# Attention ahead of two feed-forward layers: weight tiles two passes later, six biases on another engine, three units' scores in other banks

## The chip, the core and the metric

The kernel runs on one core of a Trainium2 chip. A core has five engines that each work through a queue of their own in order: TensorE (PE; matrix products and transposes into PSUM banks, with its weight loads shown as PEld), VectorE (DVE), ScalarE (ACT), GpSimd (POOL) and SyncE (SP), which here only issues transfers. They wait for each other by semaphores. The metric is the device time of one execution in microseconds.

## The reference

Three things in a row, with 4 x 576 = 2304 tokens, 8 heads of 64, model width 512 and hidden width 2048:

```python
scores = scale * q @ k.T                       # per batch and head
scores = where((rel >= 0) & (rel < 128), scores + slopes * -abs(rel), -1e9)
attn = exp(scores - max);  attn = attn / (sum(attn) + 1e-9);  x = attn @ v
h = x @ w_in;   g = where(h > 0, h, exp(min(h, 0)) - 1);  x = g @ w_out    # layer 0
h = x @ w2_in;  g = h / (1 + exp(-h));                    out = g @ w2_out # layer 1
```

The inputs are float64; the kernel receives them as pairs of 32-bit words and must turn each weight into floats itself. It works with split numbers: a value is a high half (rounded) plus a low half (value minus high), and a product is three matmuls (high x high, high x low, low x high).

## The kernel before, in words

**Attention (lines 329 to 706).** Two neighbouring groups of 128 tokens (t) and a pair of heads (hp) are one unit; there are 36, numbered u, four head pairs to a t. The main loop (line 644) makes one turn, here called a pass, for each u from 0 to 38, and works on several units at once. In pass u:

- TensorE computes the scores of unit u (line 501; from unit 16 on line 504, with split numbers), for even u the value products of units u-4 and u-3 (line 585), and the transposes of unit u-2 (line 542).
- VectorE adds the bias to the scores and takes the maximum (line 518, "reduction"), inverts the sums of unit u-1 (lines 526 and 527) and copies half of the transposes of unit u-2 (line 553).
- ScalarE takes the exponentials of unit u (line 523), copies the value products (line 591) and the other half of the transposes (line 555).
- GpSimd normalizes unit u-1 (line 566) and, later on, copies keys (line 110).

The score banks are `s0` and `s1`, one each (line 496), so a unit's scores wait until the reduction of the unit before has read its bank. The bias of head h (line 437) is made from `rel`: heads 0 and 1 ahead of the loop, the others three each in passes 0 and 1 (line 696), all on VectorE.

**Weight tiles.** `weight_step` (line 190) works through a list of tasks, one per tile of 512 x 128 weights: load (line 118, SyncE), `rescale` (GpSimd and ScalarE), `sign` and `join` (VectorE, lines 149 and 154), `part` (ScalarE makes the high half, line 162; VectorE the difference, line 167, which is the low half, run from `owed`). It is called twice in each pass that is in the list `WSLOTS`; `u + 1` in the call is how many tasks may be loaded by then. In passes 0 to 14 the ten tiles of the first sweep come (five of `w_in`, then five of `w_out`), in passes 26 to 33 three more.

**Fill.** When the attention of a block of tokens is done, its feed-forward work is put into the list `fill`: five hidden tiles (`h`, line 244, four pieces each), then four output groups (`y`, line 302, five pieces each). Block 0 has 256 tokens, the others 512. Each pass puts in some pieces at three points (`PIECES`), strictly in order of the list; a piece is held back while its weights are not in `known` (line 693), and then all behind it wait too. A hidden tile is followed by four steps: ScalarE's exponential (line 251), VectorE's two steps (257, 258), ScalarE's high half (266) and VectorE's low half `gl` (272), which the y pieces read. The splits of a block's input into high and low (`split_x`, lines 227 and 228) stand at the end of the passes in which its value products come: 4 and 6 for block 0, 12 and 14 for block 1, 20 and 22 for block 2, 28 and 30 for block 3, two splits (a pair) in each.

**After attention (line 708).** The rest of `fill`, and then all further steps, run back to back on TensorE.

Of the kernel before, what the change touches and what calls it, by code (L numbers as in the profile page):

```python
# [8 lines left out]
F32 = mybir.dt.float32  # L9
# [5 lines left out]
ALU = mybir.AluOpType  # L15
PSUM = bass.MemoryType.PSUM

P = 128
# [24 lines left out]
def attention_elu_silu_kernel(  # L43
# [14 lines left out]
    nc = tc.nc  # L58
    NT, DM = out.shape
    B, H, S, D = shape  # L60
# [5 lines left out]
    scale = 1.0 / float(D) ** 0.5  # L66
# [17 lines left out]
    LAG = 2  # L84
    NR = 4
    PLAIN = 16
    WSLOTS = [*range(15), *range(26, 34)]
    PIECES = (2, 1, 2)
    BANKS = 3
    UNITS = [(t, hp) for t in range(NG // 2) for hp in range(NPAIR)]  # L90
# [12 lines left out]
    ps_ms = [ctx.enter_context(tc.tile_pool(name="ps_m", bufs=BANKS, space=PSUM))]  # L103
# [86 lines left out]
    def weight_step(loaded=0, which=(4, 2, 3, 1), lag=1, last=64, apart=(1, 0, 1)):  # L190


        for i in which:
            if (stage[i] < min(last, stage[i - 1]) and (i < len(stages) or fits(stage[i]))
                    and calls[0] >= at[i - 1][stage[i]] + (lag, *apart)[i - 1]):
                if i == len(stages):
                    made[tasks[stage[i]][0]] += 1
                stages[i - 1](*tasks[stage[i]])
                at[i][stage[i]] = calls[0]
                stage[i] += 1  # L200
        while stage[0] < (loaded or min(stage[-1] + NRAW, len(tasks))):
            load_w(*tasks[stage[0]])
            at[0][stage[0]] = calls[0]
            stage[0] += 1
# [124 lines left out]
    def attention():  # L329

        with ExitStack() as actx:
# [6 lines left out]
            ps_s = actx.enter_context(tc.tile_pool(name="ps_s", bufs=1, space=PSUM))  # L338
# [85 lines left out]
            rel = store[1][0][:, 0, 0:2 * P]  # L424
# [7 lines left out]
                clear(i, nc.gpsimd)  # L432
            bias = const.tile([P, H, 2 * P], BF16, tag="bias", name="bias")

            def make_bias(h):

                nc.vector.tensor_scalar(bias[:, h, :], rel, -(2.0 ** (-8.0 * (h + 1) / H)) / scale, None, op0=ALU.mult)

            make_bias(0)
            make_bias(1)  # L440
            cuts = {}

            def make_cuts():
# [44 lines left out]
            def scores(u):  # L488
                t, hp = UNITS[u]
                z, zq = kk[hp], qs.pop(u, None)  # L490
                pt = ps_[u] = p_p.tile([P, 2, 2, 2 * P], F32, tag="p", name="p")
                neg = st_p.tile([P, 4], F32, tag="neg", name="neg")
                sm = sums[u] = st_p.tile([P, 2, 2], F32, tag="sm", name="sm")
                es = []
                for j in range(2):
                    ps = ps_s.tile([P, 2, 2 * P], F32, tag=f"s{j}", name=f"s{j}")
                    for e in range(2):
                        c0 = first_col(2 * t + e)
                        cut = 2 * t + e in MID
                        if u < PLAIN:  # L500
                            nc.tensor.matmul(ps[:, e, c0:2 * P], qz[:, u % 4, j, e * P:(e + 1) * P],  # L501
                                             kz[:, u % 4, e * P + c0:(e + 2) * P], start=True, stop=not cut)
                        for x in range(0 if u < PLAIN else 2):
                            nc.tensor.matmul(ps[:, e, c0:2 * P], zq[:, j, e * P:(e + 1) * P],  # L504
                                             z[:, x, j, e * P + c0:(e + 2) * P], start=(x == 0), stop=(x == 1 and not cut))
                        if cut:
                            nc.tensor.matmul(ps[:, e, c0:2 * P], ident16, cuts[MID[2 * t + e]][:, c0:2 * P],
                                             start=False, stop=True)
                    for e in range(2):
                        g = 2 * t + e  # L510
                        i = 2 * j + e
                        c0 = AFTER.get(g, first_col(g))
                        src = ps[:, e, c0:2 * P]
                        dst = pt[:, j, e, c0:2 * P]
                        if g in AFTER:

                            nc.vector.memset(pt[:, j, e, 0:c0], 0.0)
                        nc.vector.tensor_tensor_reduce(  # L518
                            dst, src, bias[:, 2 * hp + j, c0:2 * P], -scale, 3.0e38, ALU.add, ALU.min,
                            neg[:, i:i + 1])  # L520
                        es.append((dst, neg[:, i:i + 1], sm[:, e, j:j + 1]))
                for dst, m, a in es:
                    nc.scalar.activation(dst, dst, AF.Exp, bias=m, scale=-1.0, accum_out=a)  # L523
# [120 lines left out]
            for u in range(NU + 3):  # L644
                known.update(weights)
                calls[0] += 1
                last = 2 * FIRST_F + (u >= 20) * NRAW
                if u in WSLOTS:
                    weight_step(min(u + 1, last), (4, 1), 2, last)
                pop()  # L650
                if u < NU:
                    scores(u)
# [3 lines left out]
                while owed:  # L656
                    owed.pop(0)()
                if u in WSLOTS:
                    weight_step(min(u + 1, last), (2, 3), 1, last)
                pop()  # L660
                evict = keep = None
                if u % 2 == 0 and u >= 4:
# [30 lines left out]
                                made_ready += [group(hidden(bi, f), 1, n, lambda i, f=f: (0, 0, f) in known)] * NKC  # L693
                            made_ready += outputs_of(bi)
                split_q(u + 2)
                if u < 2:
                    for h in range(2 + 3 * u, 5 + 3 * u):
                        make_bias(h)
                if u == 3:
                    make_cuts()  # L700
                point(PIECES[2])
# [114 lines left out]
```

## Time and profile before

| | |
|---|---|
| median of three runs | 923.42 us (923.14 to 923.63) |
| the profiled execution | 923.78 us, its span 922.1 us |
| busy in the span: PE, DVE, ACT, POOL | 909.7, 572.3, 434.0, 228.7 us |
| chain that ended last | PE 88%, DVE 4%, issue 3%, POOL 2%, ACT 2%, DMA 1% |
| largest lines of that chain | y L302 40%, h L244 39% |

A row of a timeline gives start and length of an instruction (or of several of the same kind that follow each other, with xN), its engine, line, operation and tiles (out<-in); in brackets stands how long the engine was idle before it and which instruction ended that wait. On TensorE each float32 product of scores, transposes and values is recorded as two. Instructions that overlap in the pipeline have lengths that add up to more than the time they take; the difference of two starts is the safer measure.

### The profile page before, as it was taken

To read this page: it belongs to the slowest core of one execution; us is meant where nothing else is said; L and a number is where in the kernel's file an instruction comes from. 1 tells how busy PE (TensorE), PEld (TensorE's weight loads), DVE (VectorE), ACT (ScalarE), POOL (GpSimd) and SP (SyncE) were. 2 spreads that over 40 slices of the span, in tenths; PEclk is the share of its full clock that TensorE was granted. 3 is DMA by queue.
4 is the path that set the end of the run, shared out by engine and by line. 5 is a ranking of instruction groups with operands and counts; after the bars stand their busy time and mean duration, and the time that the engine had idled before them with its cause. 6 is when DMAs were issued, how large, how long until landed. Compare 5 with 4: busy or idle time off the path is not lost.

```text
span 922.1 us, 12993 instructions
## 1 busy us (share of the span) xinstructions
PE 909.7 (99%) x4754; PEld 760.6 (82%) x4754; DVE 572.3 (62%) x1186; ACT 434.0 (47%) x959; POOL 228.7 (25%) x316
## 2 busy tenths in 40 slices
PE   7999999999999999999999999999999999999998
PEld 5878888887878888889888888888888888888887
DVE  7996888893777776576555556644366554444422
ACT  7776677764555434333343255543533342233311
POOL 5543555553444202220012022220221021000000
PEclk9999999999999999999999999999999999999999
DMA  9534335320242202210002012210221010000011
GB/s 271 184 100 114 103 99 173 99 64 10 90 130 91 69 1 70 69 46 1 1 17 76 23 46 71 71 43 23 69 69 47 1 46 0 35 35 23 23 46 46
DMA packets 45247, 59.81 MB, mean 65 GB/s; under 512 B 3328, under 2 KB 38912, under 8 KB 45184
## 3 DMA queue, kind: packets, MB, share of 16 engines
q1 hardware_dynamic: 45024, 58.86, 20.7%
q8 instruction: 37, 0.61, 0.3%
q14 instruction: 26, 0.21, 0.1%
q10 hardware_dynamic: 160, 0.13, 0.1%
HBM read 54.26 MB, written 4.72 MB: 64 GB/s over the span
## 4 chain that ended last, share of the span: by engine, by line
PE 88%; DVE 4%; issue 3%; POOL 2%; ACT 2%; DMA 1%; SPq 0%; POOLq 0%; DVEq 0%; ACTq 0%
PE y L302 40%; PE h L244 39%; PE a L585 3%; PE pt L542 3%; PE s L501 2%; PE s L504 2%; POOL wl L164 1%; POOL wraw L142 1%; DVE p L518 1%; DMA y<-in_k_dram 1%; DVE gl L272 0%; DMA wraw<-in_moe_w_in_dram 0%; ACT p L523 0%; DVE wraw L154 0%; DVE e L257 0%
## 5 line engine op out<-in xcount | busy, mean ns | idle before, releaser
L244 PE MATMUL h<-xh,wh 128*128 128x512 f32 (+1 forms) x640 | 238.6, 373 | 0.0
L244 PE MATMUL h<-xl,wh 128*128 128x512 f32 (+1 forms) x640 | 235.9, 369 | 0.6 <-DVE xl L228 0.6
L244 PE MATMUL h<-xh,wl 128*128 128x512 f32 (+1 forms) x640 | 235.8, 368 | 0.0
L164 POOL TENSOR_TENSOR wl<-wraw,wh 128x512 fp32r<-128x512 f32 x54 | 75.6, 1402 | 401.3 <-ACT wh L162 401.3
L272 DVE TENSOR_TENSOR gl<-e,gh 128x512 fp32r<-128x512 f32 (+1 forms) x158 | 106.0, 671 | 105.0 <-ACT gh L266 104.7
L251 ACT ACTIVATE e<-h 128x512 f32<-128x512 f32 (+1 forms) x160 | 87.9, 550 | 174.5 <-PE h L244 153.5
L266 ACT ACTIVATE gh<-e 128x512 fp32r<-128x512 f32 (+1 forms) x160 | 94.0, 587 | 107.6 <-DVE e L258 65.0
L244 PEld LDWEIGHTS h<-xh,wh 128*128 128x128 f32 x640 | 120.8, 189 | 20.4 <-issue 1.2
L244 PEld LDWEIGHTS h<-xl,wh 128*128 128x128 f32 x640 | 120.8, 189 | 20.0 <-DVE xl L228 0.8
L244 PEld LDWEIGHTS h<-xh,wl 128*128 128x128 f32 x640 | 120.6, 188 | 20.1
L302 PE MATMUL y<-gh,wh 128*128 128x512 f32 (+1 forms) x320 | 121.3, 379 | 0.2 <-ACT y L310 0.2
L302 PE MATMUL y<-gl,wh 128*128 128x512 f32 (+1 forms) x320 | 118.4, 370 | 1.0 <-DVE gl L272 1.0
L302 PE MATMUL y<-gh,wl 128*128 128x512 f32 (+1 forms) x320 | 118.0, 369 | 0.0
L302 PE MATMUL y<-wh,gh 128*128 128x512 f32 (+1 forms) x294 | 113.3, 385 | 0.0
L302 PE MATMUL y<-wl,gh 128*128 128x512 f32 (+1 forms) x294 | 113.2, 385 | 0.0
L302 PE MATMUL y<-wh,gl 128*128 128x512 f32 (+1 forms) x294 | 113.2, 385 | 0.0
L566 POOL TENSOR_SCALAR p<-p,sm 128x256 f32<-128x256 f32 (+2 forms) x144 | 71.0, 510 | 98.8 <-DVE sm L527 61.2
L260 DVE TENSOR_TENSOR e<-h,e 128x512 f32<-128x512 f32 (+1 forms) x80 | 50.9, 637 | 60.4 <-ACT e L251 59.8
L162 ACT ACTIVATE wh<-wraw 128x512 fp32r<-128x512 f32 x58 | 38.5, 667 | 91.0 <-DVE wraw L154 66.7
L523 ACT ACTIVATE p<-p,neg 128x256 f32<-128x256 f32 (+2 forms) x144 | 68.9, 481 | 20.1 <-DVE neg L518 18.9
L302 PEld LDWEIGHTS y<-gh,wh 128*128 128x128 f32 x320 | 60.4, 189 | 11.6 <-issue 1.0
L302 PEld LDWEIGHTS y<-gl,wh 128*128 128x128 f32 x320 | 60.4, 189 | 11.3 <-DVE gl L272 2.0
(76 smaller groups left out, 1195.3 us busy)
## 6 DMA issues: line engine op xcount, KB each, us to landing
wraw<-in_moe_w_in_dram SPq DMA_DIRECT2D x30, 512.0 KB, 3.8
wraw<-in_moe_w_out_dram SPq DMA_DIRECT2D x28, 512.0 KB, 3.3
qr<-in_q_dram SPq DMA_DIRECT2D x40, 128.0 KB, 3.2
v<-in_v_dram SPq DMA_DIRECT2D x18, 256.0 KB, 2.9
out_dram<-x SPq DMA_DIRECT2D x17, 256.0 KB, 2.0
kr<-in_k_dram SPq DMA_DIRECT2D x32, 128.0 KB, 3.0
y<-in_k_dram SPq DMA_DIRECT2D x6, 384.0 KB, 4.7
y<-in_q_dram SPq DMA_DIRECT2D x14, 128.0 KB, 4.1
```

The source lines that it names most:

```text
L162: nc.scalar.activation(h, f32(top), AF.Copy)
L164: nc.gpsimd.tensor_tensor(lo, f32(top), f32(h), op=ALU.subtract)
L244: nc.tensor.matmul(tiles["ps"][:, 0:w], a[:, cs], b2[:, c, 0:w], start=(c == 0 and x == 0), stop=(c == NKC - 1 and x == 2))
L251: nc.scalar.activation(e[:, 0:w], tiles["ps"][:, 0:w], AF.Exp if layer == 0 else AF.Sigmoid)
L260: nc.vector.tensor_tensor(e[:, 0:w], ps[:, 0:w], e[:, 0:w], op=ALU.mult)
L266: nc.scalar.activation(gh[:, 0:w], tiles["e"][:, 0:w], AF.Copy)
L272: eng.tensor_tensor(gl[:, 0:w], tiles["e"][:, 0:w], f32(gh[:, 0:w]), op=ALU.subtract)
L302: nc.tensor.matmul(tiles["ps"][:, s], a[:, cs], b2[:, s], start=(f == f0 and x == 0), stop=(f == f1 - 1 and x == 2))
L523: nc.scalar.activation(dst, dst, AF.Exp, bias=m, scale=-1.0, accum_out=a)
L542: nc.tensor.transpose(ps[:, 2 * P * e + c:2 * P * e + c + P], pt[:, j, e, c:c + P], ident)
L566: nc.gpsimd.tensor_scalar(dst, dst, by, 1.0, op0=ALU.mult, op1=ALU.mult)
L585: nc.tensor.matmul(ps[j * D:(j + 1) * D, i, q0:q1], vv[hp // 2][(g // 2) % 2][:, g % 2, i * P + j * D:i * P + (j + 1) * D], ptt[:, j, a * ...
```

## The change

Weight tiles start in pass 2 instead of 0: `WSLOTS` begins with passes 2 to 16, and the number of tasks that may be loaded is `u - 1`. The biases of heads 2 to 7 are made by GpSimd ahead of the loop, right behind its clearing of two buffers; those of heads 0 and 1 stay on VectorE. The scores of units 1, 3 and 5 go to the three banks of `h` and `y` (`ps_ms`, three in turn) instead of `s0` and `s1`.

```diff
--- before.py
+++ after.py
@@ -84,7 +84,7 @@
     LAG = 2
     NR = 4
     PLAIN = 16
-    WSLOTS = [*range(15), *range(26, 34)]
+    WSLOTS = [*range(2, 17), *range(26, 34)]
     PIECES = (2, 1, 2)
     BANKS = 3
     UNITS = [(t, hp) for t in range(NG // 2) for hp in range(NPAIR)]
@@ -432,12 +432,12 @@
                 clear(i, nc.gpsimd)
             bias = const.tile([P, H, 2 * P], BF16, tag="bias", name="bias")
 
-            def make_bias(h):
-
-                nc.vector.tensor_scalar(bias[:, h, :], rel, -(2.0 ** (-8.0 * (h + 1) / H)) / scale, None, op0=ALU.mult)
-
-            make_bias(0)
-            make_bias(1)
+            def make_bias(h, eng):
+
+                eng.tensor_scalar(bias[:, h, :], rel, -(2.0 ** (-8.0 * (h + 1) / H)) / scale, 1.0, op0=ALU.mult, op1=ALU.mult)
+
+            for h in range(H):
+                make_bias(h, nc.vector if h < 2 else nc.gpsimd)
             cuts = {}
 
             def make_cuts():
@@ -493,7 +493,11 @@
                 sm = sums[u] = st_p.tile([P, 2, 2], F32, tag="sm", name="sm")
                 es = []
                 for j in range(2):
-                    ps = ps_s.tile([P, 2, 2 * P], F32, tag=f"s{j}", name=f"s{j}")
+                    if u < 6 and u % 2:
+
+                        ps = ps_ms[0].tile([P, 4 * P], F32, tag="m", name=f"s{j}").rearrange("p (e t) -> p e t", e=2)
+                    else:
+                        ps = ps_s.tile([P, 2, 2 * P], F32, tag=f"s{j}", name=f"s{j}")
                     for e in range(2):
                         c0 = first_col(2 * t + e)
                         cut = 2 * t + e in MID
@@ -646,7 +650,7 @@
                 calls[0] += 1
                 last = 2 * FIRST_F + (u >= 20) * NRAW
                 if u in WSLOTS:
-                    weight_step(min(u + 1, last), (4, 1), 2, last)
+                    weight_step(min(u - 1, last), (4, 1), 2, last)
                 pop()
                 if u < NU:
                     scores(u)
@@ -656,7 +660,7 @@
                 while owed:
                     owed.pop(0)()
                 if u in WSLOTS:
-                    weight_step(min(u + 1, last), (2, 3), 1, last)
+                    weight_step(min(u - 1, last), (2, 3), 1, last)
                 pop()
                 evict = keep = None
                 if u % 2 == 0 and u >= 4:
@@ -693,9 +697,6 @@
                                 made_ready += [group(hidden(bi, f), 1, n, lambda i, f=f: (0, 0, f) in known)] * NKC
                             made_ready += outputs_of(bi)
                 split_q(u + 2)
-                if u < 2:
-                    for h in range(2 + 3 * u, 5 + 3 * u):
-                        make_bias(h)
                 if u == 3:
                     make_cuts()
                 point(PIECES[2])
```

Below are the orders of instructions at three places; lines of the changed kernel are up to four higher from line 498 on.

SyncE, the first transfers, in the kernel before (`wraw` are raw weights, `y_83` the keys, `y_84` the queries, `v` the values):

```order
L371 DMA y_83<-in_k_dram 128x2x256
L394 DMA y_84<-in_q_dram 64x2x256 x2
L129 DMA wraw<-in_moe_w_in_dram 128x4x256
L405 DMA v_118<-in_v_dram 128x2x256
L129 DMA wraw<-in_moe_w_in_dram 128x4x256
L394 DMA y_84<-in_q_dram 64x2x256 x2
L371 DMA y_83<-in_k_dram 128x2x384
```

and in the changed kernel:

```order
L371 DMA y_83<-in_k_dram 128x2x256
L394 DMA y_84<-in_q_dram 64x2x256 x2
L405 DMA v_118<-in_v_dram 128x2x256
L394 DMA y_84<-in_q_dram 64x2x256 x2
L371 DMA y_83<-in_k_dram 128x2x384
L129 DMA wraw<-in_moe_w_in_dram 128x4x256
```

The queries and keys of units 4 and 5 now stand ahead of the first weight transfer instead of behind two.

VectorE, the end of pass 20, in the kernel before, up to the first reduction of pass 21 (`sm` the inversion, `ptt<-pt` the copies of transposes, `xl` the pair of splits, `p,neg` the reduction):

```order
L526 TENSOR_SCALAR sm<-sm 128x4
L527 RECIPROCAL sm<-sm 128x4
L553 COPY ptt<-pt 128x256
L553 COPY ptt<-pt 128x128
L228 TENSOR_TENSOR xl<-x_78,xh 128x512 x2
L518 ISA p,neg<-s_1583,bias 128x256
```

and in the changed kernel:

```order
L530 TENSOR_SCALAR sm<-sm 128x4
L531 RECIPROCAL sm<-sm 128x4
L272 TENSOR_TENSOR gl<-e,gh 128x512
L557 COPY ptt<-pt 128x256
L557 COPY ptt<-pt 128x128
L257 TENSOR_SCALAR e<-e 128x512
L258 TENSOR_TENSOR e<-h,e 128x512
L228 TENSOR_TENSOR xl<-x_78,xh 128x512 x2
L522 ISA p,neg<-s_1541,bias 128x256
```

The low half of the third hidden tile of block 1 and the two steps of the fourth (`e`) stand in pass 20 now, ahead of the pair of splits; they stood in pass 18.

VectorE, the second half of pass 29, in the kernel before (`qs` and `k_116` low halves of queries and keys, `wraw` sign and join):

```order
L484 TENSOR_TENSOR qs<-qr,qs 64x512
L471 TENSOR_TENSOR k_116<-kr,k_116 128x2x256
L149 SCALAR_TENSOR_TENSOR wraw<-wraw 128x512
L154 SCALAR_TENSOR_TENSOR wraw<-wraw 128x512
L526 TENSOR_SCALAR sm<-sm 128x4
L527 RECIPROCAL sm<-sm 128x4
L553 COPY ptt<-pt 128x512
```

and in the changed kernel:

```order
L484 TENSOR_TENSOR qs<-qr,qs 64x512
L471 TENSOR_TENSOR k_116<-kr,k_116 128x2x256
L149 SCALAR_TENSOR_TENSOR wraw<-wraw 128x512
L154 SCALAR_TENSOR_TENSOR wraw<-wraw 128x512
L272 TENSOR_TENSOR gl<-e,gh 128x512
L530 TENSOR_SCALAR sm<-sm 128x4
L531 RECIPROCAL sm<-sm 128x4
L257 TENSOR_SCALAR e<-e 128x512
L258 TENSOR_TENSOR e<-h,e 128x512
```

The low half of the fourth hidden tile of block 2, which stood in pass 27, now stands behind the sign and join of pass 29, and a pair of splits stands in pass 28 ahead of it.

## Rows read from the trace of the kernel before

**Rows 1.** The page: span; busy time, share and instructions of each engine.
```profile
span 922.1 us, 12993 instructions
...
PE 909.7 (99%) x4754; PEld 760.6 (82%) x4754; DVE 572.3 (62%) x1186; ACT 434.0 (47%) x959; POOL 228.7 (25%) x316
```

**Rows 2.** Busy time by stretch, columns as in the first row.
```profile
core 0: us, PE busy (x) PEld busy (x) DVE busy (x) ACT busy (x) POOL busy (x), PEclk, DMA share, GB/s
3.40:28.00 24.60, 21.64 (x120) 15.72 (x121) 21.33 (x89) 20.27 (x70) 13.69 (x30) 1.00 1.03 303
28.00:57.40 29.40, 27.77 (x204) 23.18 (x203) 27.44 (x96) 23.14 (x71) 13.69 (x26) 1.00 0.41 124
57.40:75.70 18.30, 18.30 (x150) 16.17 (x149) 13.89 (x46) 13.94 (x43) 9.20 (x18) 1.00 0.30 88
```

**Rows 3.** Chain that ended last, passes 12 and 13: start, length, what.
```profile
57.57 1.74 PE s L501 x8
...
59.67 1.94 PE a L585 x24
61.61 1.02 PE pt L542 x8
62.64 1.73 PE s L501 x8
```

**Rows 4.** Timeline of TensorE, scores of unit 4 (columns as explained above).
```profile
15.12 1.97 PE L501 MATMUL s<-y,y 128*128 128x256 f32 x8 [1.31 <-DMA y<-in_k_dram]
```

**Rows 5.** Timeline of VectorE (DVE): first biases, first sign, start of reduction 5.
```profile
6.96 0.69 DVE L437 TENSOR_SCALAR bias<-y 128x256 bf16<-128x256 f32 x3
...
13.50 0.98 DVE L149 SCALAR_TENSOR_TENSOR wraw<-wraw 128x512 uint32<-128x512 uint32 x1
...
21.70 0.41 DVE L518 CUSTOM_DVE_ANT_0 p<-s,bias 128x256 f32<-128x256 f32 x1
```

**Rows 6.** Timeline of GpSimd (POOL): normalization of unit 0.
```profile
9.30 1.78 POOL L566 TENSOR_SCALAR p<-p,sm 128x128 f32<-128x128 f32 x4 [4.89 <-DVE bias L437]
```

**Rows 7.** Timeline of VectorE, pass 11: reduction, difference, sign, inversion, next reduction.
```profile
55.99 0.41 DVE L518 CUSTOM_DVE_ANT_0 p<-s,bias 128x256 f32<-128x256 f32 x1
...
57.26 0.99 DVE L167 TENSOR_TENSOR wl<-x,wh 128x512 fp32r<-128x512 f32 x1
58.17 0.70 DVE L149 SCALAR_TENSOR_TENSOR x<-x 128x512 uint32<-128x512 uint32 x1
...
59.52 0.16 DVE L526 TENSOR_SCALAR sm<-sm 128x4 f32<-128x4 f32 x1
...
60.38 0.41 DVE L518 CUSTOM_DVE_ANT_0 p<-s,bias 128x256 f32<-128x256 f32 x1
```

**Rows 8.** Timeline of TensorE, pass 19: fourth hidden tile of block 1.
```profile
105.38 0.47 PE L302 MATMUL y<-gh,wh 128*128 128x512 f32 x1
106.30 0.50 PE L302 MATMUL y<-gl,wh 128*128 128x512 f32 x1 [0.44 <-DVE gl L272]
```

**Rows 9.** Timeline of VectorE, passes 19 and 20: low half, first split.
```profile
105.56 0.68 DVE L272 TENSOR_TENSOR gl<-e,gh 128x512 fp32r<-128x512 f32 x1
...
114.21 0.91 DVE L228 TENSOR_TENSOR xl<-x,xh 128x512 fp32r<-128x512 f32 x1 [0.81 <-ACT xh L227]
```

**Rows 10.** Timeline of VectorE, passes 27, 28, 30: low half, two split pairs.
```profile
156.01 0.68 DVE L272 TENSOR_TENSOR gl<-e,gh 128x512 fp32r<-128x512 f32 x1
...
165.37 2.15 DVE L228 TENSOR_TENSOR xl<-x,xh 128x512 fp32r<-128x512 f32 x2 [0.89 <-ACT xh L227]
...
178.67 1.28 DVE L228 TENSOR_TENSOR xl<-x,xh 128x512 fp32r<-128x512 f32 x2
```

**Rows 11.** Timeline of TensorE, pass 27: fourth hidden tile of block 2.
```profile
156.46 0.48 PE L302 MATMUL y<-gh,wh 128*128 128x512 f32 x1
156.78 0.48 PE L302 MATMUL y<-gl,wh 128*128 128x512 f32 x1
```

**Rows 12.** Timeline of GpSimd, pass 28: a key copy.
```profile
166.05 0.94 POOL L110 TENSOR_SCALAR k<-kr 128x512 fp32r<-128x512 f32 x1
```

## The prediction

> **What bounds the kernel now.** I read the page first: TensorE is recorded busy for 909.7 of the 922.1 us [rows 1]. The reader is to see that nearly the whole time is matrix work that the change neither adds nor removes, so a new time can only come from TensorE's waits. Next I read the busy time by stage [rows 2]. Up to 28.0 us TensorE is idle for 2.96 us of the stretch, from 28.0 to 57.4 us for 1.63, and from 57.4 to 75.7 us for nothing. In the first two stretches VectorE is busy for 21.33 of 24.60 us and 27.44 of 29.40 us: there the front of the kernel goes at VectorE's pace, and behind it at TensorE's. Two things follow. All that the front can give back is about 4.6 us. And once TensorE is full, a pass that asks more of VectorE than before turns straight into a wait of TensorE. So after the front I looked at every place behind it where TensorE waits for VectorE, and at the order of the instructions there.
>
> I call one turn of the main loop a pass, and number it by its u (0 to 38). In pass u VectorE reduces the scores of unit u, makes one weight tile (sign, join, difference), inverts the sums of unit u-1 and copies out the transposes of unit u-2.
>
> **The front, part by part.** Weight tiles are made two passes later, by the same instructions. So the state in which TensorE becomes full, pass 12 before, is reached in pass 14, and two more passes of attention lie ahead of it. They cost TensorE two scores of 1.73 us, two transposes of 1.02 and one set of value products of 1.94 [rows 3]: 7.4 us. In the kernel before, VectorE starts the reduction of pass 12 at 60.38 us [rows 7]; break-even is therefore that the reduction of pass 14 starts at 60.38 + 7.4 = 67.8 us.
>
> What goes from passes 0 to 4 on VectorE: two groups of three biases, one at 6.96 us with 0.61 us to the next start and a second like it (1.2 together), and two signs (the first 0.98 us [rows 5]), two joins and one difference, which at the prices of pass 11 below are 2.26 + 1.35 = 3.6. From these 4.8 us the start does not follow at once, since another chain runs beside it: GpSimd normalizes unit 0 from 9.30 us for 1.78 us [rows 6], TensorE transposes and goes on to the scores of the next pass, and ScalarE takes four exponentials per unit. With the transfers of weights no longer ahead of it in SyncE's queue, the scores of unit 4 do not wait for their key transfer; before they start at 15.12 us, after a wait of 1.31 [rows 4]. GpSimd ends unit 0 at 11.08 and unit 1, as long again, at about 12.8; the last transposes of unit 1 behind it take some 0.6, so the scores of unit 4 start at about 13.4, 1.7 us sooner. Reduction 5, before at 21.70 us [rows 5], is bounded by 16.9 (all 4.8 us gone) and 20.4 (the key transfer's 1.31 alone). I take 19.7, the 1.7 us of the scores and 0.3 more, nearer to the upper end because the chain and not VectorE sets these passes.
>
> From there VectorE is the bound. Before, passes 5 to 11 take 60.38 - 21.70 = 38.7 us. Now passes 5 to 13 hold the same weight work plus two attention shares, one difference with sign and join, one further sign and join, and one split of an input block (it stands in pass 12). Pass 11 shows the prices [rows 7]: it is 4.39 us long (55.99 to 60.38), of which 2.26 from the start of the difference to the end of the join (57.26 to 59.52), 1.35 of them for sign and join (from 58.17), so 2.13 for attention; without the zeroing that pass 11 has I count 2.2. With a pair of splits at 1.28 [rows 10] that is 4.4 + 2.26 + 1.35 + 1.28 = 9.3 us, and 19.7 + 38.7 + 9.3 = 67.7 us. VectorE's own waits in the old stretch, 1.96 us at most [rows 2], need not come back, since one hidden tile per pass replaces two. From 19.7 that is 65.7 to 67.7, and I take 67.2, near the upper end: a gain of 0.6 us. With the bounds of reduction 5 it is 62.9 to 68.4: a gain of 4.9 to a loss of 0.6 (beyond that lies rival 3).
>
> **The biases on GpSimd.** GpSimd has no bias in the trace. Its normalization of tiles of 128 and 256 columns is the nearest row, four in 1.78 us [rows 6], so six biases are some 2.7 us; by VectorE's 0.2 each they would be 1.2. Either way they lie in GpSimd's idle 4.89 us ahead of 9.30 [rows 6], and the first two are made before reduction 1, which in the kernel before follows the biases of 6.96 us [rows 5]. I cost them at nothing; without that cover each late bias would delay a reduction by at most 0.5 us.
>
> **The scores in the banks of h and y.** Units 1, 3 and 5 no longer need the bank of the unit before. In the trace the transposes and not the bank set the start of these scores, so I take 0; it can give no more than the first stretch's idle less the wait for the keys, 2.96 - 1.31 = 1.65 us [rows 2, 4]. No h tile needs a bank before pass 7, and reduction 5 has read its scores by about 21 us, so the cost is 0 too.
>
> **Behind the front: two new waits.** Matrix work of the hidden layer is put in as fill, two passes later than before against the attention units. But the splits of an input block (L228) hang on the units and stay in passes 20, 22, 28 and 30, and the signs and joins of the next three weights stay in 29 to 31. Before, VectorE finished the last hidden tiles of a block in pass 19 (and 27), and the split came in pass 20 (and 28). Now the last hidden tiles fall in passes 20 and 21 (28 and 29), on top of the split.
>
> Pass 21: already before, TensorE waited in the same place of pass 19. The y matmul that reads the low half of the fourth hidden tile starts 0.92 us after the one ahead of it (105.38 to 106.30 [rows 8]), since VectorE begins that low half only at 105.56 us [rows 9]; in pass 27 the same step is 0.32 us [rows 11], so 0.6 us are lost. VectorE has no slack there, so a split ahead of it adds its own time. A pair is 1.28 us in one row, 2.15 in another [rows 10]. VectorE's wait of 0.81 us ahead of the split in the old pass 20 [rows 9] is gone, since the hidden tile now fills it.
>
> Pass 29: before, in pass 27, the fourth low half started at 156.01 us, took some 0.6 and was read at 156.78 without a wait [rows 10, 11]; nothing was to spare. Now the split (1.28 to 2.15) and a sign and a join (1.35) stand ahead of it: 2.6 to 3.5 us.
>
> Together 3.9 to 5.7 us (from 1.28 + 2.6 to 2.15 + 3.5); I take 4.8, since the split has company on GpSimd in both passes. The long row, at 165.37, lies beside a key copy of GpSimd, 0.94 us at 166.05 [rows 10, 12], and such copies are there in passes 20 and 28 of the changed kernel too. The Trainium skill, "SBUF — State Buffer", section "Who interferes with whom", says that a VectorE instruction with two SBUF inputs and a GpSimd instruction that reads SBUF exclude each other; the split is of that kind, and the long row agrees. By that rule the sum would go to the upper end, 923.42 - 0.6 + 5.7 = 928.5 us; without it to the lower, 926.7.
>
> **The sum.** The profiled execution took 923.78 us for its span of 922.1, 0.36 above the median of 923.42. 923.78 - 0.6 + 4.8 = 928.0, which is 927.6 us against the median: that is my forecast.
>
> **The rivals.**
> 1. The late splits stay hidden and only the front counts. For it speaks that VectorE is busy for only 62% of the span [rows 1], and that it waited 0.81 us before the old split [rows 9]; against it, that TensorE already lost 0.6 us there without a split. Time: 923.42 - 0.6 = 922.8; at the most, with all recorded idle of the front gone, 923.42 - 4.6 = 918.8. This is the case on the faster side; it decides if the fourth low half of pass 21 starts no more than 0.1 us after TensorE asks for it.
> 2. Only one of the two waits comes, for instance because TensorE was held up in pass 21 and VectorE stays ahead from then on. Time: 923.42 - 0.6 + 1.3 to 3.5 = 924.1 to 926.3.
> 3. The front loses as well. Passes 7 to 13 give TensorE only one hidden tile or a single y step each, so it cannot fill a wait there; and if each of the nine passes 5 to 13 loses 0.25 us beside GpSimd, as a difference of 0.99 us does against a sign of the same size at 0.70 [rows 7], reduction 14 comes 2.2 us late, at 69.4 us. Time: 923.42 + 1.6 + 4.8 = 929.8 us, 930.7 with the upper end behind it.
>
> **How the numbers follow.** My forecast (both waits, the front about even) gets 0.62, with a range of its own from 925 to 929.5; rival 1 gets 0.17, rival 2 0.13, rival 3 0.08. A measurement tells some 0.2%, 1.85 us, from no change: below 921.6 is faster, above 925.3 slower. Rival 1 gives 0.09 to faster and 0.08 to the same; rival 2 and the low edge of the forecast give 0.11 more to the same; the rest, 0.72, is slower. The range for 8 in 10 goes from 923.0, which leaves out most of rival 1, to 931.0.
>
> **What would show it.** Right: reduction 5 near 19.7 us; TensorE at the scores of pass 14 near 64 us; in pass 21 a y matmul waiting for a low half by 2 to 3 us, in pass 29 by 2.6 to 3.5, each with a split ahead of it on VectorE. Wrong: no wait of TensorE above 1 us between 100 and 200 us (rival 1), or scores of pass 14 after 66 us (rival 3).

## The result, and the profile after

The changed kernel took 935.53 us (median of 933.54, 934.23, 936.82 and 937.47) against 923.37 us of the kernel before: 1.0131 times as long, 95% interval 1.0106 to 1.0157. Forecast were 927.6 us and 923.0 to 931.0: the sign was right, the size was not.

In the rows of the changed kernel lines of the attention are four higher (reduction L522, inversion L530 and L531, copies L557, transposes L546, scores L505 and L508, normalization L570). The page first, answering to [rows 1]: the matrix work is the same, the span is 9.3 us longer.

```profile
span 931.4 us, 12994 instructions
...
PE 911.7 (98%) x4754; PEld 763.1 (82%) x4754; DVE 569.7 (61%) x1180; ACT 435.8 (47%) x959; POOL 232.0 (25%) x322
```

**The front.** VectorE, start of reduction 5 (before at 21.70 us, [rows 5]):

```profile
18.49 1.16 DVE L228 TENSOR_TENSOR xl<-x,xh 128x256 fp32r<-128x256 f32 x2 [0.90 <-ACT xh L227]
19.58 0.41 DVE L522 CUSTOM_DVE_ANT_0 p<-s,bias 128x256 f32<-128x256 f32 x1
```

Forecast was 19.7. The scores of unit 4, forecast at 13.4 us, start at 13.18, and the six biases take GpSimd 2.46 us of its idle time. Next GpSimd's normalization of unit 11 in pass 12, in the kernel before and in the changed one, and VectorE's pair of splits beside the second:

```profile
64.26 2.68 POOL L566 TENSOR_SCALAR p<-p,sm 128x256 f32<-128x256 f32 x4 [2.44 <-DVE sm L527]
...
58.72 2.69 POOL L570 TENSOR_SCALAR p<-p,sm 128x256 f32<-128x256 f32 x4 [2.79 <-DVE sm L531]
59.02 1.32 DVE L228 TENSOR_TENSOR xl<-x,xh 128x512 fp32r<-128x512 f32 x2
```

TensorE of the changed kernel, the scores and the transposes of pass 13 and the scores of pass 14:

```profile
56.21 1.89 PE L505 MATMUL s<-y,y 128*128 128x256 f32 x8
...
59.26 0.44 PE L546 MATMUL pt<-ident,p 128*128 128x128 f32 x2 [0.81 <-POOL p L570]
60.61 1.54 PE L546 MATMUL pt<-ident,p 128*128 128x128 f32 x6 [0.91 <-POOL p L570]
61.95 3.33 PE L505 MATMUL s<-y,y 128*128 128x256 f32 x8
```

The normalization is long because the pair of splits of pass 12 lies beside it on VectorE: in experiments 4 and 9, where the pair goes to GpSimd or one pass later, the same normalization takes 1.73 and 1.74 us. It was as long in the kernel before. New is that TensorE waits for it, twice: between the scores and the transposes of pass 13 it had eighteen y matmuls then, and has three now. Then eight scores take 3.33 us instead of 1.89 one pass earlier: TensorE's clock.

**The clock.** Busy time by stretch, columns as in [rows 2]; PEclk is the granted clock, 1.00 for 2.4 GHz and 0.50 for 1.2.

```profile
61.43:64.84 3.41, 3.41 (x10) 2.84 (x10) 3.34 (x9) 2.52 (x8) 1.05 (x2) 0.50 0.00 0
64.84:70.00 5.16, 5.16 (x46) 4.31 (x45) 4.32 (x15) 4.05 (x12) 2.81 (x8) 1.00 0.20 60
110.00:120.00 10.00, 7.43 (x46) 6.15 (x47) 8.49 (x26) 6.48 (x22) 4.08 (x8) 0.83 0.18 52
112.63:116.04 3.41, 3.41 (x11) 2.95 (x12) 2.84 (x6) 2.03 (x5) 2.94 (x6) 0.50 0.52 153
```

Twice TensorE runs at the lower level for 3.41 us, each time behind waits: the two above, and the one of pass 21 below. In the profile of the kernel before the clock stays at 1.00 from 7.1 to 921.9 us. The mean granted clock was 0.996, 0.994, 0.993 and 0.993 in the four runs, in the order of their times; in 51 runs of the kernel before, beside the experiments, it was 0.998 to 1.000.

**Passes 21 and 29.** TensorE, the y matmuls of the fourth hidden tile (before: [rows 8, 11]):

```profile
108.92 0.47 PE L302 MATMUL y<-gh,wh 128*128 128x512 f32 x1
112.57 0.77 PE L302 MATMUL y<-gl,wh 128*128 128x512 f32 x1 [3.18 <-DVE gl L272]
...
165.16 0.47 PE L302 MATMUL y<-gh,wh 128*128 128x512 f32 x1
169.05 0.50 PE L302 MATMUL y<-gl,wh 128*128 128x512 f32 x1 [3.41 <-DVE gl L272]
```

The interval between two such matmuls is 0.23 us where nothing disturbs them; so 3.42 and 3.66 us are lost, against 0.69 and 0.09 before. At these two places that is 6.3 us more. VectorE at the same places:

```profile
106.98 2.12 DVE L228 TENSOR_TENSOR xl<-x,xh 128x512 fp32r<-128x512 f32 x2
109.02 0.41 DVE L522 CUSTOM_DVE_ANT_0 p<-s,bias 128x256 f32<-128x256 f32 x1
...
110.50 0.69 DVE L484 TENSOR_TENSOR qs<-qr,qs 64x512 fp32r<-64x512 f32 x1
111.22 0.69 DVE L471 TENSOR_TENSOR k<-kr,k 128x512 fp32r<-128x512 f32 x1
111.83 0.69 DVE L272 TENSOR_TENSOR gl<-e,gh 128x512 fp32r<-128x512 f32 x1
...
162.27 2.08 DVE L228 TENSOR_TENSOR xl<-x,xh 128x512 fp32r<-128x512 f32 x2
...
166.98 0.69 DVE L149 SCALAR_TENSOR_TENSOR wraw<-wraw 128x512 uint32<-128x512 uint32 x1
167.70 0.69 DVE L154 SCALAR_TENSOR_TENSOR wraw<-wraw 128x512 uint32<-128x512 uint32 x1
168.31 0.69 DVE L272 TENSOR_TENSOR gl<-e,gh 128x512 fp32r<-128x512 f32 x1
```

VectorE never rests from the split to the low half, and the low half that TensorE asks for comes last. Both pairs of splits take the long price, beside these key copies of GpSimd:

```profile
106.92 0.62 POOL L110 TENSOR_SCALAR k<-k 128x512 fp32r<-128x512 f32 x1
107.63 0.93 POOL L110 TENSOR_SCALAR k<-kr 128x512 fp32r<-128x512 f32 x1
...
162.17 0.61 POOL L110 TENSOR_SCALAR k<-k 128x512 fp32r<-128x512 f32 x1
162.87 0.93 POOL L110 TENSOR_SCALAR k<-kr 128x512 fp32r<-128x512 f32 x1
```

**Behind the main loop** there are waits that the prediction does not have. TensorE, y pieces of the last block (block 4; experiment 3 below calls it block 3):

```profile
249.56 0.39 PE L302 MATMUL y<-gh,wl 128*128 128x512 f32 x1
250.78 0.50 PE L302 MATMUL y<-gh,wh 128*128 128x512 f32 x1 [0.83 <-ACT gh L266]
251.51 0.50 PE L302 MATMUL y<-gl,wh 128*128 128x512 f32 x1 [0.22 <-DVE gl L272]
```

VectorE ahead of them:

```profile
243.12 1.08 DVE L149 SCALAR_TENSOR_TENSOR wraw<-wraw 128x512 uint32<-128x512 uint32 x1
244.24 1.66 DVE L154 SCALAR_TENSOR_TENSOR wraw<-wraw 128x512 uint32<-128x512 uint32 x1
245.82 0.41 DVE L257 TENSOR_SCALAR e<-e 128x512 f32<-128x512 f32 x1
```

Sign and join (2.7 us) stand ahead of the steps of this block's hidden tiles. They come early because the list `fill` is not empty when the main loop ends: ten y pieces of block 3 are left, before none. `layers` puts them in and calls a weight step at every second one.

**The sum by stretch.** For every matmul I take the time to the start of the next one less what its kind takes undisturbed in the kernel before, and add that up; a change of kind costs a little even on a full TensorE, so only differences count. In us:

| stretch | before | changed | no left steps | splits later | low first | three repairs | five repairs | before, low first |
|---|---|---|---|---|---|---|---|---|
| to 100 us | 26.29 | 25.06 | 25.39 | 25.42 | 25.21 | 24.87 | 25.85 | 26.06 |
| 100 to 140 | 6.23 | 10.38 | 8.89 | 7.32 | 7.74 | 7.43 | 6.59 | 5.61 |
| 140 to 180 | 6.98 | 9.96 | 11.45 | 9.04 | 8.54 | 7.93 | 7.69 | 6.53 |
| 180 to 230 | 7.93 | 7.91 | 7.89 | 7.86 | 7.86 | 7.74 | 6.39 | 7.91 |
| 230 to 320 | 1.55 | 5.16 | 1.33 | 4.93 | 5.23 | 1.29 | 1.56 | 1.51 |
| the rest | 1.38 | 1.22 | 1.18 | 1.17 | 1.20 | 1.21 | 1.19 | 1.17 |

Changed less before: -1.23 + 4.15 + 2.98 - 0.02 + 3.61 - 0.16 = 9.33 us, the difference of the spans. The other columns are the experiments below.

The first four rows are safe only together. The changes of kind come in clusters, and the changed kernel is passes ahead at the same time (reduction 18 at 87.05 us against 97.47), so a row gains or loses a cluster by where its edge lies: changed less before is +0.8 us up to 95 us, -0.2 up to 98, -1.2 up to 100 and -0.2 up to 102. Up to 230 us this evens out. There the changed kernel has lost 5.88 us more than the kernel before; no left steps 6.19, splits later 2.21, low first 1.92, three repairs 0.54, five repairs -0.91, low first in the kernel before -1.32.

### The profile page after: what moved, and what is told of

The parts are those of the page before. It is cut to its first block, busy times and chain, and to the rows that moved or that the text cites. A ratio compares the mean times of both kernels' runs of the same rounds, so it can differ in the third digit from the quotient of the medians.

```text
span 931.4 us, 12994 instructions
## 1 busy us (share of the span) xinstructions
PE 911.7 (98%) x4754; PEld 763.1 (82%) x4754; DVE 569.7 (61%) x1180; ACT 435.8 (47%) x959; POOL 232.0 (25%) x322
## 4 chain that ended last, share of the span: by engine, by line
PE 82%; DVE 9%; issue 3%; POOL 2%; ACT 2%; DMA 1%; POOLq 0%; DVEq 0%; ACTq 0%
PE y L302 38%; PE h L244 36%; PE a L589 2%; PE pt L546 2%; PE s L508 2%; DVE p L522 2%; PE s L505 1%; POOL wl L164 1%; DMA wraw<-in_moe_w_in_dram 1%; DVE wraw L154 1%; DVE wraw L149 1%; DVE gl L272 1%; DVE e L257 1%; DVE e L258 1%; ACT gh L266 1%
## 5 line engine op out<-in xcount | busy, mean ns | idle before, releaser
L570 POOL TENSOR_SCALAR p<-p,sm 128x256 f32<-128x256 f32 (+2 forms) x144 | 71.0, 511 | 97.1 <-DVE sm L531 57.3
L302 PEld LDWEIGHTS y<-gl,wh 128*128 128x128 f32 x320 | 60.6, 189 | 19.4 <-DVE gl L272 10.2
```

The source lines that it names most:

```text
L302: nc.tensor.matmul(tiles["ps"][:, s], a[:, cs], b2[:, s], start=(f == f0 and x == 0), stop=(f == f1 - 1 and x == 2))
L570: nc.gpsimd.tensor_scalar(dst, dst, by, 1.0, op0=ALU.mult, op1=ALU.mult)
```

## The experiments

Each was timed beside the kernel before; ratios are against those runs (median 923.74 to 923.82 us). The intervals in brackets are 95%.

**1. The weights alone**

```diff
 (kernel before)
-    WSLOTS = [*range(15), *range(26, 34)]
+    WSLOTS = [*range(2, 17), *range(26, 34)]
-                    weight_step(min(u + 1, last), ...   (both calls)
+                    weight_step(min(u - 1, last), ...
```

> The kernel before with one part of the change, the weight tiles two passes later; biases and banks stay as before. Theory: the delay of the weights makes all of the new waits (3.4 us in pass 21, 3.7 in pass 29, some 3.3 in the stretch from 245 to 310 us) and with them the stretches at half clock, 3.4 us each, that the profile of the changed kernel shows behind its waits. Then this kernel is within 2 us of the changed one: 933.5 to 938, and the waits of passes 21 and 29 are each over 3 us. Rival: the six biases on GpSimd or the other banks carry a share of the loss; then this one is more than 3 us faster than the changed kernel, under 932.

936.72 us (933.43 to 938.08), ratio 1.0136 [1.0116, 1.0156]; waits of 3.45 us in pass 21 and 3.65 in pass 29. The whole loss, the half clock too, comes with the weights. The profiled run, the longest, has two stretches of 6.83 us at half clock, which begin 1.2 and 0.6 us before these waits end. Up to 230 us it has lost 10.2 us more than the kernel before, against 5.9 of the changed kernel's profile: 4.3 us for 10.2 us more at half clock behind the two waits, some 1.4 for each 3.41.

**2. Biases and banks alone**

```diff
 (changed kernel)
-    WSLOTS = [*range(2, 17), *range(26, 34)]
+    WSLOTS = [*range(15), *range(26, 34)]
-                    weight_step(min(u - 1, last), ...   (both calls)
+                    weight_step(min(u + 1, last), ...
```

> The kernel before with the other two parts of the change, six biases on GpSimd and the scores of units 1, 3 and 5 in the banks of h and y; the weights stay in passes 0 to 14. Theory: both are free behind the front, and in the front they give back at most the 2.96 us of idle time of TensorE up to 28 us; VectorE sheds 1.2 us of biases: 922.2 to 923.4, no wait over 1 us between 100 and 200 us, granted clock 1.000. Rival: the long normalizations or the biases on GpSimd make the front later: over 924.

923.83 us (922.85 to 925.37), ratio 1.0003 [0.9993, 1.0012]: nothing, and not the 922.2 to 923.4 us that were expected. The longest of these runs is the profiled one, where the clock fell in the front, after a stretch in which TensorE was busy for 3.91 of 6.50 us (columns as above):

```profile
10.00:16.50 6.50, 3.91 (x23) 2.93 (x23) 4.84 (x18) 5.64 (x21) 5.15 (x12) 1.00 1.11 301
16.52:19.93 3.41, 3.41 (x16) 2.12 (x16) 2.06 (x9) 2.98 (x9) 1.62 (x4) 0.50 1.12 264
```

**3. No weight steps among the left pieces**

```diff
 (changed kernel, layers)
-                if i % 2:
-                    calls[0] += 1
-                    weight_step(0, lag=LAG)
                 continue
```

> The changed kernel without the weight steps that are called while the ten y pieces left over from the main loop are put in. Theory: these five extra calls bring raw weights, signs and joins into VectorE's queue ahead of the low halves of block 3, and make the waits of y matmuls for low halves from 245 to 310 us (4.35 us against 1.08 before). Without them these waits fall under 1.5 us and the time falls by some 3 us, to 930.5 to 934.5. Rival: the waits come from the ten late pieces themselves, or from the later start of the layers; then they stay at over 3 us and the time stays at 933.5 to 937.5.

931.20 us (929.98 to 932.89), ratio 1.0082 [1.0067, 1.0098]. From 230 to 320 us 1.33 us are lost instead of 5.16: the extra calls, not the ten pieces, make these waits (for the low halves of block 4). The run shows the price of the clock too, since up to 230 us it runs the same instructions as the changed kernel. From 100 to 140 us it stays at the full clock and loses 8.89 us, the changed kernel 10.38 with one stretch at half clock; from 140 to 180 us it is the other way round, 11.45 with (169.28 to 172.69 us) and 9.96 without. A stretch of 3.41 us thus costs 1.49 us, both times. The one at 61.43 us costs less: the changed kernel, ahead of this run from the first passes on, starts reduction 14 0.93 us sooner (64.72 against 65.65), and reduction 18 still 0.43 us sooner (87.05 against 87.48). That is 0.5 us, where VectorE sets the pace.

**4. Splits on GpSimd**

```diff
 (changed kernel, split_x)
-        nc.vector.tensor_tensor(xl[:, c, 0:w], ...
+        eng = nc.gpsimd if i in (1, 2) and c < 2 else nc.vector
+        eng.tensor_tensor(xl[:, c, 0:w], ...
```

> The changed kernel with the low halves of the pairs of splits in passes 20 and 28 made by GpSimd instead of VectorE (four instructions). Theory: the pair, 2.1 us in each pass, stands ahead of the late low half on VectorE. Without it the wait of pass 21 falls from 3.4 to about 1.3 us and that of pass 29 from 3.7 to about 1.6, 4.2 together, and if the half clock behind pass 21 comes from that wait, 1.7 more goes: 929.5 to 932. Rival: VectorE is slowed beside GpSimd by as much, or the chain in pass 21 starts at the reduction and not at the split; then both waits stay over 2.5 us and the time over 933.

934.34 us (933.81 to 934.90), ratio 1.0113 [1.0096, 1.0130]. The edit was not quite what the text says: it moves the pairs of passes 12 and 20; that of pass 28 stayed, and its wait with it (3.61 us). In pass 21 the wait is 3.26 us instead of 3.43. VectorE and then GpSimd (lines one higher):

```profile
108.84 1.66 DVE L485 TENSOR_TENSOR qs<-qr,qs 64x512 fp32r<-64x512 f32 x1
110.53 1.64 DVE L472 TENSOR_TENSOR k<-kr,k 128x512 fp32r<-128x512 f32 x1
```

```profile
108.66 2.96 POOL L229 TENSOR_TENSOR xl<-x,xh 128x512 fp32r<-128x512 f32 x2
```

Two instructions of 0.69 us take 1.66 and 1.64 beside the pair: 1.9 of the 2.1 us are lost again. The rival was right for pass 21; that VectorE's pair was on the path is not refuted by it, only paid for in another way. The profile has a stretch at half clock behind each of the two waits.

**5 and 6. Splits one pass later; low half first**

```diff
 (5: changed kernel; run at the end of passes 21 and 29)
-        nc.vector.tensor_tensor(xl[:, c, 0:w], ...
+        low = lambda: nc.vector.tensor_tensor(xl[:, c, 0:w], ...
+        if i in (2, 3) and c < 2: later.append(low)
+        else: low()
```

```diff
 (6: changed kernel)
+                if u in (21, 29): pop()
                 low_q(u + 1)
                 low_k(u + 1)
                 ...
-                pop()
+                if u not in (21, 29): pop()
```

> The changed kernel with the pairs of splits of passes 20 and 28 queued on VectorE one pass later, behind the late low half (nothing goes to another engine). In the run with splits on GpSimd the two instructions for queries and keys took 1.66 and 1.64 us instead of 0.69 each beside them, and gave back what the split had freed. Theory: without that company the wait of pass 21 falls from 3.4 to 1.3 us and that of pass 29 from 3.7 to 1.6, so 4.2 us go, and up to 1.7 us for each stretch at half clock that follows such a wait: 928.5 to 932.5. Rival: the wait is set by the reduction and the query and key work between the scores and the low half alone; then both waits stay over 2.5 us and the time over 933.

> The changed kernel with the low half queued on VectorE ahead of the low halves of queries and keys (and of sign and join) in passes 21 and 29; the splits stay where they are. Theory: the wait is the sum of what stands between the scores and the low half on VectorE. Of it 1.4 us (query and key) go in pass 21 and 2.7 us (with sign and join) in pass 29: waits of 2.0 and 0.9 us, 4.1 together off the time, 929 to 932.5. Rival: the low half waits for its high half on ScalarE rather than for its turn; then the waits move by less than 0.5 us each and the time stays over 933.

930.03 us (929.39 to 931.41), ratio 1.0070 [1.0055, 1.0085], and 929.62 us (929.42 to 930.37), ratio 1.0065 [1.0050, 1.0080]. TensorE in pass 21, of 5 and then of 6:

```profile
109.11 0.47 PE L308 MATMUL y<-gh,wh 128*128 128x512 f32 x1
110.68 0.50 PE L308 MATMUL y<-gl,wh 128*128 128x512 f32 x1 [1.09 <-DVE gl L278]
```

```profile
109.15 0.47 PE L302 MATMUL y<-gh,wh 128*128 128x512 f32 x1
111.34 0.50 PE L302 MATMUL y<-gl,wh 128*128 128x512 f32 x1 [1.72 <-DVE gl L272]
```

Less the 0.23 us these are waits of 1.34 and 1.97 us (expected 1.3 and 2.0), in pass 29 1.76 and 0.84 (1.6 and 0.9). So the wait falls by what is taken out of VectorE's queue ahead of the low half, term by term. Neither profile has a stretch at half clock inside the kernel (over all eight runs the mean is 0.996 to 1.000), and three of four runs of each lie within 0.7 us. The mean does not give the time by itself: in 5 the longest run has 1.000, and the run with 0.996 lies in the middle.

**7. Three repairs** (3, 5 and 6 together)

> The changed kernel with three repairs together: splits one pass later, low half first in passes 21 and 29, and no weight steps among the ten left y pieces. Theory: no wait over 0.8 us is left between 100 and 320 us, so that the front's gain of some 1.3 us shows, and with no long wait no stretch at half clock from 70 us on: 921.5 to 923.5, at or a little under the kernel before. Rival 1: the half clock has nothing to do with the waits; then it still shows in most runs and the time is 924 to 928. Rival 2: the moved work makes new waits of the same size; then 926 or more.

924.84 us (923.88 to 925.29), ratio 1.0012 [1.0003, 1.0022]. The long waits are gone, none over 0.6 us is left from 100 to 230 us, but no gain shows: up to 230 us the profile has lost 0.54 us more than the kernel before. The 1.3 us of the theory were read off the row up to 100 us, which depends on its edge. The time is where rival 1 has it, but not for its reason: only four of ten runs have a mean clock below 1.000, and the profiled one, with half clock at 61 us alone, is the shortest. New waits as in rival 2 could only be small and many; where they lie is open.

**8. A wait in the kernel before**

```diff
 (kernel before)
+            scr = const.tile([P, 48], F32, ...   (ahead of the loop, cleared by GpSimd)
 ...
+                if u == 19:
+                    for _ in range(15):
+                        nc.vector.tensor_scalar_add(scr, scr, 1.0)
                 pop()
```

> The kernel before with a chain of fifteen small additions on VectorE, some 3 us in all, put ahead of the low half in pass 19, where the old wait of 0.7 us is; nothing else differs. It makes one wait of some 3.5 us on TensorE in the old order. Theory: such a wait is followed in most runs by a stretch at half clock of 3.4 or 6.8 us, worth 1.7 or 3.4 us, so the time is 923.7 + 2.8 + 0 to 3.4 = 926.5 to 930 and differs from run to run by more than a microsecond. Rival: the half clock belongs to the order of the changed kernel and not to a wait; then the clock stays at 1.000 behind the wait and all runs are within 0.6 us of 926.5.

928.05 us (927.79 to 929.47), ratio 1.0052 [1.0035, 1.0069]. VectorE's added work, TensorE's wait behind it, and the stretch behind that:

```profile
105.80 3.30 DVE L664 TENSOR_SCALAR scr<-scr 128x48 f32<-128x48 f32 x15
```

```profile
105.52 0.48 PE L302 MATMUL y<-gh,wh 128*128 128x512 f32 x1
109.74 0.80 PE L302 MATMUL y<-gl,wh 128*128 128x512 f32 x1 [3.74 <-DVE gl L272]
```

```profile
109.44:112.85 3.41, 3.11 (x9) 2.63 (x10) 2.74 (x8) 1.75 (x5) 2.58 (x6) 0.50 0.00 1
```

Old order, one wait of 4.0 us: in the profile the clock falls there and nowhere else. The mean clock is 0.998 in three runs and 0.996 in the longest. So the half clock belongs to the wait and does not need the new order. The lower level starts 0.3 us ahead of the matmul that ends the wait.

**9 to 12. Two more repairs; the low half first in the old kernel; one pass instead of two**

```diff
 (9: kernel of 7; the pair of pass 12 later too)
-        if i in (2, 3) and c < 2: later.append(low)
+        if i in (1, 2, 3) and c < 2: later.append(low)
-    WSLOTS = [*range(2, 17), *range(26, 34)]
+    WSLOTS = [*range(2, 17), *range(29, 37)]
 (10: kernel before, as 6, in passes 19 and 27)
 (11: changed kernel)
-    WSLOTS = [*range(2, 17), *range(26, 34)]
+    WSLOTS = [*range(1, 16), *range(26, 34)]
-                    weight_step(min(u - 1, last), ...
+                    weight_step(min(u, last), ...
 (12: 11 with the edits of 3 and 5, and of 6 in passes 20 and 28)
```

> The kernel with three repairs and two more: the pair of splits of pass 12 also goes one pass later, and the late weight slots are passes 29 to 36 instead of 26 to 33. Theory: in the profile with three repairs the front loses some 2 us in pass 13 to normalizations that take 2.7 instead of 1.8 us beside the split, and passes 28 to 31 lose some 1.5 us since VectorE is full there with signs, joins and splits. Both go: 921.5 to 923.5, under the kernel before. Rival: both stretches are full of VectorE's work whatever its order, so that what is moved is lost one pass on: 924 to 925.5, as with three repairs.

> The kernel before with the low half queued ahead of the low halves of queries and keys in passes 19 and 27, nothing else. Theory: the wait of 0.7 us in pass 19 goes and nothing takes its place: 922.8 to 923.3. Rival: the scores of the next pass wait for queries and keys that come 0.7 us later; then no change, 923.6 to 924.2.

> The changed kernel with the weight tiles one pass later than before instead of two. By the order of VectorE's work the fourth low half now stands right behind the pair of splits of pass 20 (28), but ahead of the reduction and the query and key work of the next pass, and there is no sign or join between. Theory: the wait is what stands ahead of the low half on VectorE, so it is the old wait plus at most the pair: under 2.5 us in each place, without half clock behind it; five y pieces are left, with half of the waits behind 230 us. Front about 0.7 better: 925 to 929. Rival: a shift by one pass meets the same waits as a shift by two: 932 to 938.

> The kernel with weights one pass later, and its splits of passes 20 and 28 one pass later, the low half first in these passes, and no weight steps among the left y pieces. Theory: no wait over 0.8 us from 100 to 320 us and a front gain of some 0.7 us stays: 922.5 to 924. Rival: as with two passes the gain is eaten between 100 and 200 us: 924 to 926.

9: 922.62 us (922.25 to 922.94), ratio 0.9986 [0.9977, 0.9995], in its theory's range, but not all for its reason. The normalization beside which the split had stood takes 1.74 us again, and the next one, beside which the split now stands, 2.80 instead of 1.85: the front's part was moved by a pass, as the rival has it, and up to 100 us the profile has lost no less than with three repairs (25.85 against 24.87). What is gained comes later; that the late weight slots bring it was not tried alone.

10: 922.54 us (922.32 to 922.85), ratio 0.9985 [0.9975, 0.9994], a little under its theory's range: the gain is 1.3 us and not 0.7, and by the table some 0.4 us of it lie behind 140 us. Both 9 and 10 are a little faster than the kernel before, and 13 us than the changed one; 10 needs nothing of the change.

11: 929.81 us (929.30 to 930.40), ratio 1.0062 [1.0047, 1.0077], a little above its theory's range: no wait over 0.9 us from 100 to 200 us, but one of 2.27 us at 275 us, with five pieces left, and up to 100 us some 2 us more lost than in the kernel before, where 0.7 us less was expected. 12: 924.45 us (923.68 to 926.00), ratio 1.0007 [0.9998, 1.0017], no different from before and in its rival's range; it too has lost some 2 us more up to 100 us. Both profiles have one stretch at half clock at 65 us, behind waits like those of pass 13 above. Why the front loses with one pass is open. With the waits mended, one pass (924.45 us) and two (924.84 us) come out nearly the same.

## Why the prediction was wrong in size

**The front** came out as costed at its start (scores of unit 4 at 13.18 us against 13.4, reduction 5 at 19.58 against 19.7) and better further on: reduction 14 at 64.72 against 67.2. The step "the state in which TensorE becomes full, pass 12 before, is reached in pass 14" held only in part. In the run of experiment 5, at full clock, TensorE is busy throughout pass 14, but waits 0.54 us in pass 15: there VectorE's last weight difference now meets the first low halves of queries and keys, while before it fell in pass 13, two passes ahead of them. How much of the lead of 3 us that VectorE has at reduction 14 lasts, the rows of the table do not tell to better than a microsecond; the forecast gain of 0.6 us is neither confirmed nor refuted by itself.

**Biases and banks** at nothing: right (experiment 2).

**The two waits** were right in place and cause, and too small in size: 2.7 and 3.6 us more than before at their places, where 1.28 to 2.15 and 2.6 to 3.5 were taken. The term that was mis-sized is the pair of splits, for which the sum took the middle: it cost 2.12 and 2.08 us, the long price both times. The trace of the kernel before could have settled that, since both of its own pairs in these passes are long, 2.15 us in pass 28 [rows 10], and in pass 20, of which [rows 9] show the first half:

```profile
114.21 1.93 DVE L228 TENSOR_TENSOR xl<-x,xh 128x512 fp32r<-128x512 f32 x2 [0.81 <-ACT xh L227]
```

The rule of the Trainium skill that the prediction cites ("SBUF — State Buffer", "Who interferes with whom") pointed to the long price too, and the trace agrees: both pairs lie beside GpSimd's key copies. In pass 21 the reduction is longer as well: 1.48 us from its start to the query work, against 1.22 in the old pass 19, where two of its four tiles have 128 columns.

**Front and waits together** came out near the sum, and partly by luck. Up to 230 us 5.88 us are lost, 1.49 of them by the clock behind pass 21 (experiment 3); the 4.4 that remain stand against 4.8 - 0.6 = 4.2. The waits were 1.5 us larger than taken, and the rest of the attention gave back 1.3 us more than the 0.6 of the front. Where, the runs do not show.

**What was missing** is what put the result outside the range.

- "So after the front I looked at every place behind it where TensorE waits for VectorE" was not done beyond pass 30. The fill moves as a whole, so the ten pieces at its end fall out of the main loop into code that makes weights beside them: 3.6 us (experiment 3). The order of the changed kernel shows it without a run. No term of the sum stands for it.
- The sum took a wait of TensorE at its own length. Behind those of 3.3 to 4.0 us its clock could fall, at 1.5 us for each 3.41 us in a stretch where TensorE sets the pace (experiment 3; experiment 8 shows the fall in the old order). One such stretch is in the profiled run, the shortest of the four.

With these, from the forecast: 927.6 + 0.2 (front and waits) + 3.6 + 1.5 = 932.9 us, beside the 933.54 of the profiled run. The median lies 2 us higher still. The mean clock of the other three runs is lower, 0.994 and 0.993 against 0.996, and in experiment 1 a run at 0.993 shows four times 3.41 us behind the two waits and takes 938.08 us. So more stretches at half clock are the likely reason, but no trace of these three runs shows them.

**The rivals.** 1 and 2 (one wait or none) are refuted by the rows of passes 21 and 29. Rival 3 is refuted by reduction 14 at 64.72 us and the scores of pass 14 at 61.95, though its mechanism, waits of the front beside GpSimd, exists in pass 13 (the normalization of 2.69 us).

Open stays why the clock did not fall behind the 3.66 us of pass 29 in the changed kernel's profile, while it did in those of experiments 1, 3 and 4; and why up to 230 us experiment 7 loses 1.45 us more than experiment 9, since 9 changed two things at once.

## What to carry to other kernels

Where work is shifted against a fixed schedule, follow the whole list to its end and past the loop: what falls out at the far end lands in code with other rules. On a full TensorE the length of a wait is set by the instructions that VectorE has ahead of the result asked for, so the cheapest cure is the order inside one pass; here that alone made the old kernel 0.15% faster. Moving such a pair to GpSimd shortened the wait by only 0.17 us, since both engines slowed each other. When losses are added up by stretches of time, try other edges before a row is read.

## What the runs showed of the hardware

- The granted clock of TensorE fell to half inside a kernel that keeps it busy for 98% of its span, behind single waits of 3.3 to 4.0 us, in seven of nine places in the profiles (not in pass 29 of the changed kernel and pass 21 of experiment 3); behind 2.0 us and less at the same places it did not in the profiles of experiments 5 and 6. The waits alone do not settle it: behind the two of 0.65 to 0.92 us in pass 13 it fell in the changed kernel and in experiments 7, 11 and 12, and not in 1, 3, 5 and 6, which have the same waits.
- Beside a pair of GpSimd's subtractions (1.48 us each) VectorE's subtractions took 1.65 us instead of 0.69; beside VectorE's pair of splits (1.32 us) GpSimd's normalization took 2.69 us, and the same one 1.73 and 1.74 without the pair beside it (experiments 4 and 9); beside GpSimd's key copies (0.62 and 0.93 us) it was the pair that was long, 2.12 us.
